# Sliding-window attention with a channel mix on one core: the tail loads of batch 0 moved ahead of the second run loads, and a new order of all engines

## The chip, the cores and the metric

The kernel runs on one core of a Trainium2 chip. A core has five engines that each take their own instructions strictly in the order in which the program hands them over: TensorE (PE in the profile; its weight loads are PEld), VectorE (DVE), ScalarE (ACT), GpSimd (POOL) and SyncE (SP). They wait for each other only by semaphores. SP, ACT and POOL also issue DMA transfers, which 16 DMA engines carry out. The metric is the device time of one execution in microseconds (us), lower is better.

## What is computed

Eight batches of 576 tokens go through causal attention of eight heads of 64 with a window of 128 tokens and a linear (ALiBi) bias, and then through a channel mix as in RWKV. Inputs and output are float32; the kernel works in bfloat16 with float32 sums.

```python
scores = scale * np.matmul(q, k.transpose(0, 1, 3, 2))
mask = (rel >= 0) & (rel < window)          # rel = query position - key position
scores = np.where(mask, scores + bias[None], -1000000000.0)
...
x = attention output, heads side by side     # (8, 576, 512)
x_prev = x moved on by one token
xk = mu_k * x + (1.0 - mu_k) * x_prev
xr = mu_r * x + (1.0 - mu_r) * x_prev
k = np.maximum(xk @ w_k, 0.0)                # 512 -> 1024
v = k * k @ w_v                              # 1024 -> 512
r = 1.0 / (1.0 + np.exp(-(xr @ w_r)))        # 512 -> 512
return (r * v).astype(np.float32)
```

## The kernel before

**The work of one batch.** Heads are handled in four pairs (g = 0 to 3), two pairs at a time (c = 0 and 1) from batch 1 on. For batches 1 to 7 q and k come into `raw` (line 568, four loads each batch), VectorE transposes them into `qt` (line 1157), TensorE makes the scores in two halves per c (line 1190) into the two double banks `duo`, ScalarE takes the exponential (line 1211), VectorE multiplies by a mask that holds the bias and the window (line 1224). The product with V, with a column of ones for the sum, is line 803; reciprocal and division are lines 809 and 814. For batches 1 to 3 the result goes back through TensorE (line 841) and a copy (line 717) into `xt`, with channels on the partitions; from batch 4 on a DMA of SyncE transposes it (line 889). VectorE then forms the difference to the token before (`dl`, line 867) and from it `xk` and `xr` (line 874), four channel groups each.

The channel mix is cut into row pieces: batch 0 in tokens 0 to 255 and 256 to 511, then for each pair of batches the rest. One piece needs eight blocks of line 956 (xk times w_k, four matmuls each, into one of four single banks `uno`), each followed by a relu on ScalarE (line 963) and a square on ScalarE (line 927) or VectorE (line 929), whichever the planner finds free. Then, for each 128 tokens, a block of line 974 (xr times w_r, four matmuls) with a tanh on ScalarE (line 981), two blocks of line 990 (squares times w_v, four matmuls each), and the product of both on VectorE (line 995), which SyncE sends out (line 1020).

**Batch 0 is special.** To start early, its q and k come in by small loads: tokens 0 to 255 through `qx` on the queues of SP and ACT (line 581); tokens 256 to 511 as "run" loads on GpSimd's queue (line 543), first q and k of heads 0 to 3, then of heads 4 to 7; and the last 64 tokens of all heads as two "tail" loads into `ts` (line 561). The runs are transposed on TensorE by line 1051 pair by pair, the tails by line 904 for all pairs together, after which VectorE copies them into `tt`. The second of the two score pieces of each pair in this part reads `tt` (line 747). The bias of batch 0 is added on TensorE by a product with `sid` and `dist` (line 734).

**What sets the order.** Every step is a node of a planner (class `Plan`) with engines that may run it, a cost, dependencies, buffers that it takes and gives back, and a priority. `plan.run` goes through a modelled time and starts on each engine the ready node of best priority; the nodes are then emitted in the order of their starts, and this fixes the order of the instructions on every engine, since the program is built without another scheduler. The priority of a node is its place in the pipeline plus a number from the table `NUDGE`, looked up by the node's number (`rank`, lines 432 to 444). The loads on GpSimd's queue are chained in the order of the string `LOADS` (line 220), one letter for each step of `load_step` (lines 624 to 651): `v` and `V` are halves of V of batch 0, `K` and `k` halves of w_k, `2` and `3` the runs of heads 0 to 3 and 4 to 7, `t` the tails, `a`, `b`, `c` batch 1, `R`, `W`, `w` the other weights. TensorE also gets 90 products of a zero tile (line 708), of lowest priority, wherever the planner has nothing else for it at the start.

Each load on GpSimd's queue signals one of eight semaphores in turn and, from the ninth on, waits until the load that used the same semaphore before has landed.

Of the kernel before, what the change touches and what calls it, by code (L numbers as in the profile page):

```python
# [182 lines left out]
def kernel(  # L183
# [36 lines left out]
    LOADS = 'vK23tVkabRcWw'  # L220
# [106 lines left out]
    def dve_t(n, fast=1):  # L327
# [347 lines left out]

    for what in LOADS:
        load_step(what)
# [618 lines left out]
```

## Time and profile before

| | us |
|---|---|
| median of three runs | 227.17 |
| lowest and highest | 226.61 and 227.76 |
| the profiled execution | 226.8 |
| its span in the trace | 225.0 |
| TensorE busy in it | 215.5 |

The span runs from the first to the last instruction of the trace; the execution's own time is 1.8 us longer. In the lines of the profile a group such as `L956 PE MATMUL uno<-xk,wk_sb` names the line of the kernel, the engine, what is written and what is read; in the timeline the first two numbers are start and duration in us, and the bracket says how long the engine stood idle just before and what ended that.

### The profile page before, as it was taken

To read this page: it belongs to the slowest core of one execution; us is meant where nothing else is said; L and a number is where in the kernel's file an instruction comes from. 1 tells how busy PE (TensorE), PEld (TensorE's weight loads), DVE (VectorE), ACT (ScalarE), POOL (GpSimd) and SP (SyncE) were. 2 spreads that over 40 slices of the span, in tenths; PEclk is the share of its full clock that TensorE was granted. 3 is DMA by queue.
4 is the path that set the end of the run, shared out by engine and by line. 5 is a ranking of instruction groups with operands and counts; after the bars stand their busy time and mean duration, and the time that the engine had idled before them with its cause. 6 is when DMAs were issued, how large, how long until landed. Compare 5 with 4: busy or idle time off the path is not lost.

```text
span 225.0 us, 5805 instructions
## 1 busy us (share of the span) xinstructions
PE 215.5 (96%) x2309; PEld 128.5 (57%) x2339; DVE 195.3 (87%) x378; ACT 167.9 (75%) x319; POOL 58.5 (26%) x88
## 2 busy tenths in 40 slices
PE   8999978999999999999999999999999999999994
PEld 8575736656755555464774545445674455456642
DVE  7387999999999999999998999999999966993432
ACT  3669999498998689967996997676996884527511
POOL 8758535456101900070005600190000000000000
PEclk9999999999999999999999999999999999999999
DMA  6999999999981996189354993599871315141023
GB/s 162 187 166 200 195 155 207 191 189 188 232 166 50 97 209 154 50 56 145 115 69 45 249 188 84 134 153 186 151 108 29 144 47 117 33 144 62 0 93 140
DMA packets 66298, 29.74 MB, mean 132 GB/s; under 512 B 53976, under 2 KB 58336, under 8 KB 66272
## 3 DMA queue, kind: packets, MB, share of 16 engines
q0 software_dynamic: 46832, 16.26, 66.6%
q1 hardware_dynamic: 17696, 12.53, 19.9%
q10 hardware_dynamic: 1744, 0.59, 1.1%
q8 instruction: 18, 0.29, 0.5%
q14 instruction: 8, 0.07, 0.1%
HBM read 33.56 MB, written 9.44 MB: 191 GB/s over the span
## 4 chain that ended last, share of the span: by engine, by line
PE 88%; DVE 3%; ACT 3%; DMA 3%; issue 1%; SPq 1%; DVEq 0%; ACTq 0%
PE uno L990 27%; PE uno L956 27%; PE uno L974 13%; PE duo L803 7%; PE duo L1190 6%; DMA qx<-in_q_dram 3%; PE uno L841 2%; PE uno L708 1%; PE duo L734 1%; PE uno L803 1%; DVE qt L1157 1%; PE duo L747 1%; SPq L581 1%; ACT rl L963 1%; DVE xk L874 1%
## 5 line engine op out<-in xcount | busy, mean ns | idle before, releaser
L956 PE MATMUL uno<-xk,wk_sb 128*128 128x256 bf16 (+2 forms) x410 | 70.4, 313 | 1.2 <-ACT rs L981 0.3
L990 PE MATMUL uno<-wv_sb,kk 128*128 128x512 bf16 (+2 forms) x281 | 67.1, 373 | 1.2 <-issue 0.6
L1211 ACT ACTIVATE at<-duo 128x1024 bf16<-128x1024 f32 x56 | 55.2, 1040 | 13.6 <-PE duo L1190 13.5
L963 ACT ACTIVATE rl<-uno 128x256 bf16<-128x256 f32 (+2 forms) x104 | 47.0, 478 | 12.2 <-PE uno L956 10.9
L956 PEld LDWEIGHTS <-wk_sb 128*128 128x128 bf16 x416 | 38.8, 98 | 22.8 <-issue 1.8
L990 PEld LDWEIGHTS <-kk 128*128 128x128 bf16 x296 | 27.0, 98 | 29.9 <-issue 2.3
L1224 DVE TENSOR_TENSOR at<-at,mask 128x1024 bf16<-128x1024 bf16 x56 | 37.1, 685 | 1.4 <-ACT at L1211 1.2
L547 POOL DMA_DIRECT2D vs<-in_v_dram x32 | 28.5, 905 | 36.4 <-PE duo L803 29.0
L974 PE MATMUL uno<-wr_sb,xr 128*128 128x512 bf16 x135 | 35.1, 379 | 0.5
L927 ACT ACTIVATE kk<-rl 128x256 bf16<-128x256 bf16 (+2 forms) x74 | 35.1, 517 | 0.5
L1157 DVE STREAM_TRANSPOSE qt<-raw 128x576 f32<-128x576 f32 x28 | 33.4, 1236 | 0.0
L981 ACT ACTIVATE rs<-uno 128x512 bf16<-128x512 f32 x36 | 21.6, 616 | 14.0 <-PE uno L974 13.9
L995 DVE SCALAR_TENSOR_TENSOR ot<-rs,uno 128x512 f32<-128x512 bf16 (+2 forms) x37 | 24.2, 664 | 7.6 <-ACT rs L981 4.6
L874 DVE SCALAR_TENSOR_TENSOR xr<-dl,mu_sb,xt 128x576 bf16<-128x576 bf16 (+1 forms) x32 | 24.6, 771 | 0.1
L874 DVE SCALAR_TENSOR_TENSOR xk<-dl,mu_sb,xt 128x576 bf16<-128x576 bf16 (+1 forms) x32 | 24.5, 776 | 0.1
L803 PEld LDWEIGHTS <-at 128*128 128x128 bf16 x576 | 21.4, 98 | 4.9 <-issue 0.8
L814 DVE TENSOR_TENSOR xu<-duo,rc 128x640 bf16<-128x640 f32 x28 | 22.7, 817 | 0.5 <-PE uno L841 0.3
L974 PEld LDWEIGHTS <-xr 128*128 128x128 bf16 x144 | 13.5, 98 | 14.5 <-issue 0.4
L1190 PE MATMUL duo<-qt 32*128 32x256 bf16 (+2 forms) x560 | 18.1, 250 | 1.1 <-ACT at L1211 0.9
L803 PE MATMUL duo<-vs,at 128*128 128x65 bf16 x448 | 18.8, 194 | 0.3 <-ACT at L1211 0.3
L1190 PEld LDWEIGHTS <-qt 32*128 32x128 bf16 x560 | 11.7, 92 | 11.7 <-issue 9.4
L929 DVE TENSOR_TENSOR kk<-rl 128x256 bf16<-128x256 bf16 (+2 forms) x30 | 10.0, 337 | 8.5 <-ACT rl L963 8.0
(73 smaller groups left out, 159.6 us busy)
## 6 DMA issues: line engine op xcount, KB each, us to landing
out_dram<-ot SPq DMA_DIRECT2D x34, 256.0 KB, 2.5
vs<-in_v_dram POOLq DMA_DIRECT2D x32, 128.0 KB, 9.5
raw<-in_q_dram POOLq DMA_DIRECT2D x14, 288.0 KB, 8.8
raw<-in_k_dram POOLq DMA_DIRECT2D x14, 288.0 KB, 9.3
wk_sb<-in_moe_w_k_dram POOLq DMA_DIRECT2D x2, 512.0 KB, 7.8
wv_sb<-in_moe_w_v_dram POOLq DMA_DIRECT2D x2, 512.0 KB, 11.5
qx<-in_k_dram ACTq DMA_DIRECT2D x4, 128.0 KB, 5.1
qx<-in_q_dram SPq DMA_DIRECT2D x4, 128.0 KB, 4.8
```

What stands on the lines that cost most here:

```text
L547: return dma(POOL, 256, issue_t(1024), lambda e: nc.gpsimd.dma_start(out=vs_buf[h.idx][:, j, :, 0:D], in_=v[b, :, 128 * j:128 * j + 128].r ...
L803: nc.tensor.matmul(a[:, hl, t - t0], lhsT=at[:, lo:lo + 128], rhs=vs[:, u, 2 * g + hl, :] if u < NF else tvb[:, 2 * g + hl], start=(u == u ...
L874: lambda e: nc.vector.scalar_tensor_tensor(out=buf[hk.idx][:, g, e0 + c0:e0 + c1], in0=dls(), scalar=mu[:, g:g + 1], in1=xc(1), op0=ALU.mu ...
L927: nc.scalar.activation(out=out, in_=in_, func=AF.Square)
L956: nc.tensor.matmul(one(hp)[:, 0:n], lhsT=wk_sb[:, po, 128 * fo:128 * fo + 128], rhs=xk_buf[hx.idx][:, po, c0:c1], start=(po == 0), stop=(p ...
L963: a = op(ACT, act_t(n), [s], pr, lambda e, hp=hp, hr=hr: nc.scalar.activation(out=rl_buf[hr.idx][:, 0:n], in_=one(hp)[:, 0:n], func=AF.Rel ...
L974: nc.tensor.matmul(one(hp), lhsT=xr_buf[hx.idx][:, po, 128 * c:128 * c + 128], rhs=wr_sb[:, po], start=(po == 0), stop=(po == NPO - 1))
L990: nc.tensor.matmul(one(hv)[:, a:b], lhsT=kk_buf[hk.idx][:, fo, o:o + 128], rhs=wv_sb[:, fo, a:b], start=(fo == 0), stop=(fo == NFO - 1))
L1157: nc.vector.transpose(out=qt_buf[hq.idx][:, S * i:S * i + S].rearrange("p s t -> p (s t)").bitcast(FP32) .rearrange("p (q t) -> p t q", t=TB),
L1190: nc.tensor.matmul(two(hps[j // 2])[:, j % 2, c0:c0 + n], lhsT=qt[r:r + 32, S + 128 * u:S + 128 * u + 128, t], rhs=qt[r:r + 32, q0:q0 + n, t],
L1211: lambda e, ah=ah, j=j: nc.scalar.activation(out=ah(), in_=two(hps[j]), func=AF.Exp, scale=float(scale)), (), [hps[j]])
L1224: nc.vector.tensor_tensor(out=a, in0=a, in1=m, op=ALU.mult)
```

## The change

Two things are changed and nothing else. In `LOADS` the letter `t` moves ahead of `3`: the tail loads of batch 0 are issued between the two pairs of its run loads. And the table `NUDGE` is replaced by another (931 entries before, 865 after, 4 of them equal). The nodes, their costs and their dependencies stay, but for the chain of the four loads that change places.

```diff
-    LOADS = 'vK23tVkabRcWw'
+    LOADS = 'vK2t3VkabRcWw'
...
     NUDGE = {
-        647: 9.44, 648: 14.18, 650: 28.28, 651: -0.02, 652: 28.26, 654: 14.18, 655: 14.18, 656: -0.02, 657: 4.7, 658: 23.5, 659: 14.12, 660: 9.48,
-        661: 4.72, 662: -4.8, 663: 4.72, 664: -4.82, 665: 14.14, 666: -4.82, 667: 9.46, 668: 9.42, 669: 9.38, 670: 28.24, 671: 9.42, 672: 18.76,
...
+        649: 9.36, 650: 4.76, 651: 9.36, 652: -0.02, 653: 0.02, 654: 4.72, 655: -0.04, 656: 9.3, 657: 18.78, 659: 28.22, 660: -4.72, 661: -4.72,
+        662: 4.64, 663: 0.04, 665: 0.02, 666: 4.58, 667: -4.74, 668: -4.76, 669: 4.64, 671: 14.14, 672: -4.76, 673: -0.04, 674: 14.14, 675: -0.1,
...
     }
```

With this the order of instructions is another on TensorE, VectorE, ScalarE and SyncE from the fifth microsecond on; on GpSimd only the four loads change places. TensorE keeps the same number of each kind of instruction. VectorE has 384 steps of the planner instead of 378 and ScalarE 317 instead of 323, since squares and copies may go to either. Line numbers of the new program are five lower behind the table; in this text all lines are those of the kernel before.

147 rows, old and new, of the table NUDGE are left out of this document.

## The prediction

> **What bounds the kernel now.** First the page: busy shares, the 40 slices and the chain that ended last.
>
> ```profile
> span 225.0 us, 5805 instructions
> PE 215.5 (96%) x2309; PEld 128.5 (57%) x2339; DVE 195.3 (87%) x378; ACT 167.9 (75%) x319; POOL 58.5 (26%) x88
> ...
> PE   8999978999999999999999999999999999999994
> ...
> DVE  7387999999999999999998999999999966993432
> ACT  3669999498998689967996997676996884527511
> ...
> PE 88%; DVE 3%; ACT 3%; DMA 3%; issue 1%; SPq 1%; DVEq 0%; ACTq 0%
> ```
>
> TensorE carries 88% of the chain, and only its first slices are not full. To see where it is not, the view by stretches (columns: PE, PEld, DVE, ACT, POOL busy, clock, DMA):
>
> ```profile
> 15.00:26.00 11.00, 10.29 (x187) 6.43 (x186) 9.66 (x27) 10.56 (x29) 6.68 (x10) 1.00 1.39 192
> 26.00:33.20 7.20, 5.89 (x94) 3.83 (x89) 7.12 (x14) 7.13 (x15) 2.73 (x5) 1.00 2.08 161
> 33.20:43.00 9.80, 8.87 (x138) 6.46 (x140) 9.45 (x21) 7.97 (x17) 5.13 (x7) 1.00 1.24 205
> 43.00:51.20 8.20, 8.09 (x85) 4.69 (x88) 8.18 (x15) 6.05 (x11) 4.29 (x7) 1.00 1.90 184
> 51.20:221.80 170.60, 168.80 (x1659) 96.02 (x1684) 151.10 (x254) 128.80 (x237) 27.92 (x41) 1.00 0.70 117
> ```
>
> Three regimes. From 26 to 33.2 us VectorE (7.12 of 7.20) and ScalarE (7.13) are both full and TensorE is idle for 1.31 us: these two are the bound there. From 33.2 to 43 TensorE still loses 0.93. From 51.2 on it loses 1.80 in 170.6 us, about 1%. All matmuls are the same before and after, so a new order can win only idle: 0.71 + 1.31 + 0.93 + 0.11 to 51.2 us, 1.80 later, 4.9 us in all; and a delay up to 43 us reaches the end undiminished, since TensorE then has no slack to take it up. [...]
>
> **The change, part by part.** *The loads.* On GpSimd's queue the two tail loads (ts) go ahead of the second pair of run loads (raw) of batch 0. Nothing is added: the same four issues, in another order.
>
> ```profile
> 6.44 0.77 POOL L543 DMA_DIRECT2D raw<-in_q_dram  x1
> 7.17 0.78 POOL L543 DMA_DIRECT2D raw<-in_k_dram  x1
> 7.90 0.67 POOL L561 DMA_DIRECT2D ts<-in_q_dram  x1
> 9.08 0.61 POOL L561 DMA_DIRECT2D ts<-in_k_dram  x1 [0.51 <-DMA vs<-in_v_dram]
> ...
> 17.07 0.53 POOL L568 DMA_DIRECT2D raw<-in_k_dram  x1 [1.94 <-DMA raw<-in_k_dram]
> 17.33 0.32 PE L1051 MATMUL uno<-ident,raw 64*64 64x64 bf16 x16
> ...
> 17.57 0.59 PE L904 MATMUL uno<-ident,ts 128*64 128x64 bf16 x16
> ```
>
> The ninth load on GpSimd's queue waits for the landing of the first (the 0.51 us). In the new order that wait falls on the last run load: it issues at 9.08 instead of 7.17, 1.9 us later, and the tails 1.4 to 1.9 earlier. Landing is another matter: the run load landed at 17.0 (the wait of 1.94 ends with it), both tails were there at 17.57, behind it. If landing follows the order on the queue, the four swap places inside 17.6, and pairs 2 and 3 are transposed at about 17.6 instead of 17.33. Bounds: 0, and +1.9 if landing moves as far as the issue. I take 0, for the rows put all four landings within a few tenths before 17.6. What is queued behind on GpSimd are the loads of batch 1, whose first wait (1.94 us) then names a tail instead of a run; weights and V follow in the old order, so nothing later moves by this. Below zero: the tails come early, but their copies stood ready in time before, and ScalarE and VectorE, full, set the pace.
>
> *The order up to the scores of batch 1's second half.* I compared the instruction orders of both programs engine by engine. Ahead of the first L1190 of heads 4 to 7, TensorE executes the same set in both. On ScalarE the sets ahead of its exponentials differ by three small copies and squares that trade places with VectorE, about 0.05 us. As ScalarE is full there, this point stays where it is:
>
> ```profile
> 25.41 2.33 DVE L1157 STREAM_TRANSPOSE qt<-raw 128x576 f32<-128x576 f32 x2
> ...
> 29.16 1.25 DVE L1157 STREAM_TRANSPOSE qt<-raw 128x576 f32<-128x576 f32 x1
> ...
> 31.25 1.94 ACT L1211 ACTIVATE at<-duo 128x1024 bf16<-128x1024 f32 x2
> ...
> 33.25 0.64 PE L1190 MATMUL duo<-qt 32*128 32x256 bf16 x16 [0.19 <-DVE qt L1157]
> ```
>
> The new VectorE order runs the second pair of transposes back to back, which ends it at 29.16 + 2 x 1.17 = 31.5 instead of 33.2. It gains nothing: the scores also wait for both banks of the duo tiles, free when the exponentials end at 33.19.
>
> *The order from 33.9 to 43.* Here lies the difference that I can price. Before, TensorE goes on with three L956 blocks. After, it has an L974 first, which reads xr of all four pairs, and VectorE reaches the last of these after two dl, two masks, three xr and two xk.
>
> ```profile
> 33.71 1.00 DVE L874 SCALAR_TENSOR_TENSOR xk<-dl,mu_sb,xt 128x320 bf16<-128x320 bf16 x2
> 34.03 1.98 ACT L1211 ACTIVATE at<-duo 128x1024 bf16<-128x1024 f32 x2
> 34.63 3.10 DVE L1224 TENSOR_TENSOR at<-at,mask 128x1024 bf16<-128x1024 bf16 x5
> ...
> 36.06 0.64 PE L1190 MATMUL duo<-qt 32*128 32x256 bf16 x24
> ...
> 37.24 2.02 ACT L1211 ACTIVATE at<-duo 128x1024 bf16<-128x1024 f32 x2
> ```
>
> From 31.5: 2 x 0.62 for the masks, 5 x 0.50 for xr and xk, 2 x 0.30 for dl (an estimate from the 0.50 of the wider operation) make 4.3, so 35.8. TensorE, free at 33.9, waits 1.9 us, against 0.93 of idle in that stretch before: +1.0. Against it: before, ScalarE squeezes five pieces of L963 and L927 between the exponentials that end at 36.0 and those that start at 37.24; after, two. That takes back about half of 1.24, say 0.5. The blocks that TensorE does until the first transpose L841 of batch 1 are others, but worth the same:
>
> ```profile
> 41.38 0.55 PE duo L803 x18
> 41.92 0.86 PE uno L990 x4
> ...
> 45.92 0.87 PE uno L956 x8
> 46.80 0.88 PE uno L974 x4
> ```
>
> Before: six L956 at 0.44, one L974, three L803, two L990: 2.64 + 0.88 + 1.65 + 1.72 = 6.89. After: three, two, four and two: 1.32 + 1.76 + 2.20 + 1.72 = 7.00. Step: +1.0 - 0.5 = **+0.5 us**; bounds -0.9 (all idle of this stretch gone) and +1.9.
>
> *After 51 us.* Ahead of the first scores of batch 4 both orders have the same number of TensorE blocks, two exchanged. Five squares and one copy's choice of engine move to other places (L927 runs 69 times, L929 35), hidden behind TensorE. I take the 1.80 us of idle as unchanged; bounds 0 and twice that. The last five blocks of TensorE are the same, so what lies behind the last matmul stays.
>
> Sum: 226.8 for the profiled execution (span 225.0 and 1.8 around it) + 0.5 = 227.3. The median of the three runs, 227.17, is 0.37 above the profiled one, so 227.3 + 0.37 = **227.7 us**.
>
> **The rivals.** *ScalarE becomes the bound at 43 to 48 us (slower).* The new order pushes five L956 blocks between the four L841 of batch 1, ahead of the scores of batch 2; before, only two stood there.
>
> ```profile
> 39.05 1.04 ACT L963 ACTIVATE rl<-uno 128x256 bf16<-128x256 f32 x3
> 39.84 0.83 ACT L927 ACTIVATE kk<-rl 128x256 bf16<-128x256 bf16 x2
> 45.96 0.64 ACT L717 COPY xt<-uno 128x576 bf16<-128x576 bf16 x1 [0.53 <-PE uno L841]
> 51.15 0.64 PE L1190 MATMUL duo<-qt 32*128 32x256 bf16 x24
> ```
>
> TensorE needs 5 x 0.44 + 4 x 0.29 = 3.4 for them, ScalarE 4 x 0.64 + 5 x 0.35 + 5 x 0.41 = 6.4, and with four uno banks TensorE can't run far ahead. The L990 and the scores behind (0.86 and 0.6) cover 1.5 of the 3.0; the rest, 1.5, is lost: 229.2. For it: ScalarE was idle 2.15 us from 43.0 to 51.2 because its work had been done earlier, and now is not. Against: overlap of its instructions makes the true cost less (three L963 start within 0.79 us). It decides once ScalarE enters this stretch later than TensorE, that is when the wait at 33.9 exceeds my 1.9.
>
> *The new order fills the holes (faster).* L974 and L990 cost ScalarE less per microsecond of TensorE than L956, and the new order has more of them at 34 to 41. If the wait of 1.9 is no wait (xr early), 0.9 goes there and half of the 1.31 before: 227.17 - 0.9 - 0.65 = 225.6.
>
> *The later order is worse (slower).* The idle after 51.2 doubles: 227.17 + 1.8 = 229.0. For it: everything is permuted; against: the handovers keep their distances. Behind the last attention block of the last batch stand 10 blocks of TensorE instead of 12 until its first L956, but VectorE takes that block's normalisation at once instead of after several others.
>
> *The swap does harm (slower).* The run load lands 1.9 later, and ScalarE, full from 15 us, hands all of it on: 229.1. That is also how the change could fail to do what it says: the tails early, but nothing waiting for them.
>
> *The clock.* It was 1.00 in every stretch above, with 1.31 us idle in 7.2. [...]
>
> **How the numbers follow.** Forecast 0.44, ScalarE's knot 0.22, later order worse 0.10, late run load 0.06 (slower 0.38 together), holes filled 0.18. 0.5% of 227.17 is 1.1 us, about what a measurement of this kernel can tell from no change: faster is below 226.0, slower above 228.3. The forecast's own range is 226.1 to 228.3. The one for 8 in 10 takes in the rivals on both sides: 225.6 to 229.3.
>
> **What would show it.** Right: L904 ahead of the L1051 of pairs 2 and 3, those at about 17.6; the first L1190 of heads 4 to 7 at 33 to 33.6; a wait of TensorE on an xr of VectorE after it; the L1190 of batch 2 that stood at 51.15 at about 51.6, one L990 owing or not; idle after it near 1.8. Wrong: a wait for raw beyond 18.5; waits on ScalarE (rl, kk, xt) at 43 to 48; no wait at 34; over 3 us of idle after 51.

## The result, and the profile after

The changed kernel takes 229.91 us (median of 4 executions, 228.18 to 230.46); the kernel before took 227.12 beside it (226.61 to 227.76). The ratio is 1.011, 95% interval 1.0073 to 1.0147: slower, where 227.7 with a range of 225.6 to 229.3 had been forecast. The profiled execution took 229.43, its span 227.5. From here on line numbers are those of the kernel that is spoken of: in the changed one and in all that are built on it they are five lower than before (L1185 is the scores line L1190, L1206 the exponential L1211, L969 is L974, L951 is L956, L985 is L990).

The page of the changed kernel, shares and slices as before:

```profile
span 227.5 us, 5822 instructions
PE 215.9 (95%) x2309; PEld 127.8 (56%) x2339; DVE 197.1 (87%) x384; ACT 166.4 (73%) x313; POOL 59.1 (26%) x88
...
PE   7899958999999999999999999899999999999994
...
PEclk9999988999999999999999999999999999999999
...
PE 85%; ACT 5%; DMA 5%; DVE 2%; issue 1%; ACTq 1%; DVEq 0%
```

TensorE is busy for as long as before (215.9 against 215.5) in a span 2.5 us longer. New are two 8 in the row of the granted clock, in the sixth and seventh slice, and ScalarE with 5% of the chain. The same five stretches as before, the last one now up to 224 us, in the view by stretches (PE, PEld, DVE, ACT, POOL busy, clock, DMA share, GB/s):

```profile
15.00:26.00 11.00, 10.42 (x203) 7.04 (x202) 9.62 (x28) 10.56 (x29) 7.07 (x10) 1.00 1.38 193
26.00:33.20 7.20, 4.41 (x72) 2.98 (x72) 6.92 (x12) 6.43 (x15) 2.94 (x5) 0.92 2.04 159
33.20:43.00 9.80, 9.11 (x108) 5.16 (x108) 8.28 (x18) 8.05 (x13) 4.94 (x7) 0.88 1.25 205
43.00:51.20 8.20, 8.01 (x105) 5.71 (x106) 7.95 (x14) 6.82 (x18) 4.85 (x8) 1.00 1.88 193
51.20:224.00 172.80, 170.49 (x1666) 96.63 (x1691) 153.93 (x264) 127.22 (x231) 27.82 (x40) 1.00 0.71 116
```

From 26 to 33.2 us TensorE now idles for 2.79 us instead of 1.31, and ScalarE, which was full there (7.13), has 0.77 us free. From 33.2 to 43 TensorE looks busier than before (9.11 against 8.87) with fewer matmuls (108 against 138): the clock was 0.88, so each took longer. What happened is seen in the timelines (start, duration, group; the bracket is the idle time ahead and what ended it). ScalarE before:

```profile
28.55 1.99 ACT L1211 ACTIVATE at<-duo 128x1024 bf16<-128x1024 f32 x2
30.38 0.81 ACT L717 COPY xt<-uno 128x320 bf16<-128x320 bf16 x2
```

ScalarE after:

```profile
29.09 1.03 ACT L1206 ACTIVATE at<-duo 128x1024 bf16<-128x1024 f32 x1
29.99 0.44 ACT L712 COPY xt<-uno 128x320 bf16<-128x320 bf16 x1
30.30 1.06 ACT L1206 ACTIVATE at<-duo 128x1024 bf16<-128x1024 f32 x1
32.09 1.94 ACT L1206 ACTIVATE at<-duo 128x1024 bf16<-128x1024 f32 x2 [0.73 <-PE duo L1185]
```

and TensorE after:

```profile
28.13 0.64 PE L1185 MATMUL duo<-qt 32*128 32x256 bf16 x16 [0.17 <-DVE rc L804]
28.78 0.34 PE L836 MATMUL uno<-ident,xu 128*128 128x128 bf16 x3
31.41 0.64 PE L1185 MATMUL duo<-qt 32*128 32x256 bf16 x24 [2.30 <-ACT at L1206]
...
32.74 2.77 PE L969 MATMUL uno<-wr_sb,xr 128*128 128x512 bf16 x6 [0.22 <-issue]
35.44 0.65 PE L1185 MATMUL duo<-qt 32*128 32x256 bf16 x16
```

TensorE before, at the same block:

```profile
29.68 0.29 PE L1190 MATMUL duo<-qt 32*128 32x256 bf16 x2 [0.27 <-ACT at L1211]
30.59 0.64 PE L1190 MATMUL duo<-qt 32*128 32x256 bf16 x22 [0.62 <-ACT at L1211]
```

The scores of batch 1 go into two double banks, and the second scores block writes bank 0 first. Before, ScalarE emptied bank 0 and then bank 1, back to back. In the new order it empties bank 1, then makes a copy of `xt`, and then empties bank 0: the waiting block of TensorE can't start until the last of the three is done, and TensorE stands for 2.30 us, after three small matmuls, where before it waited 0.27 and 0.62. ScalarE in turn waits 0.73 us for those scores. Behind them six L969 take 2.77 us, where seven take 1.90 at full clock (e14, below). The granted clock microsecond by microsecond (PE busy, clock, DMA share, GB/s):

```profile
32.00:33.00 1.00, 0.78 (x9) 0.55 2.62 135
33.00:34.00 1.00, 1.00 (x3) 0.50 1.81 184
34.00:35.00 1.00, 1.00 (x4) 0.50 1.30 194
35.00:36.00 1.00, 1.00 (x18) 0.74 1.25 208
```

The clock is halved for 0.90 + 1 + 1 + 0.52 = 3.42 us. With that the first scores of heads 4 to 7 are at 35.44 instead of 33.25. The loads did what the forecast said; GpSimd's queue and TensorE's products with the loaded tiles:

```profile
6.35 0.67 POOL L556 DMA_DIRECT2D ts<-in_q_dram  x1
6.98 0.65 POOL L556 DMA_DIRECT2D ts<-in_k_dram  x1
...
9.32 0.77 POOL L538 DMA_DIRECT2D raw<-in_k_dram  x1 [0.91 <-DMA vs<-in_v_dram]
...
16.03 0.44 PE L899 MATMUL uno<-ident,ts 128*64 128x64 bf16 x16 [0.37 <-ACT qk L712]
17.81 0.49 PE L1046 MATMUL uno<-ident,raw 64*64 64x64 bf16 x32
```

Much later there is one more wait that was not there before: VectorE can't write an `xu` buffer of batch 5, since the DMA that transposes its last content hasn't ended, and the scores behind wait 0.74 us for it:

```profile
144.29 0.82 DVE L809 TENSOR_TENSOR xu<-duo,rc 128x640 bf16<-128x640 f32 x1 [1.33 <-DMA xt<-xu]
...
145.17 0.64 PE L1185 MATMUL duo<-qt 32*128 32x256 bf16 x16 [0.74 <-DVE xu L809]
```

### The profile page after: what moved, and what is told of

Its sections match the earlier page's. It is cut to its first block, busy times and chain, and to the rows that moved or that the text cites. A ratio compares the mean times of both kernels' runs of the same rounds, so it can differ in the third digit from the quotient of the medians.

```text
span 227.5 us, 5822 instructions
## 1 busy us (share of the span) xinstructions
PE 215.9 (95%) x2309; PEld 127.8 (56%) x2339; DVE 197.1 (87%) x384; ACT 166.4 (73%) x313; POOL 59.1 (26%) x88
## 4 chain that ended last, share of the span: by engine, by line
PE 85%; ACT 5%; DMA 5%; DVE 2%; issue 1%; ACTq 1%; DVEq 0%
PE uno L985 26%; PE uno L951 26%; PE uno L969 13%; PE duo L1185 7%; PE duo L798 6%; DMA qx<-in_k_dram 3%; DMA xt<-xu 2%; PE uno L836 2%; ACT at L1206 2%; PE uno L703 1%; PE duo L729 1%; DVE xu L809 1%; ACT xt L712 1%; PE uno L798 1%; PE duo L742 1%
## 5 line engine op out<-in xcount | busy, mean ns | idle before, releaser
L951 PE MATMUL uno<-xk,wk_sb 128*128 128x256 bf16 (+2 forms) x412 | 71.3, 313 | 0.3
L985 PE MATMUL uno<-wv_sb,kk 128*128 128x512 bf16 (+2 forms) x280 | 67.2, 373 | 0.8 <-issue 0.2
L1206 ACT ACTIVATE at<-duo 128x1024 bf16<-128x1024 f32 x56 | 55.9, 1044 | 10.2 <-PE duo L1185 10.1
L951 PEld LDWEIGHTS <-wk_sb 128*128 128x128 bf16 x416 | 38.4, 98 | 22.0 <-issue 1.2
L985 PEld LDWEIGHTS <-kk 128*128 128x128 bf16 x296 | 27.4, 98 | 30.3 <-issue 1.3
L969 PE MATMUL uno<-wr_sb,xr 128*128 128x512 bf16 x134 | 36.8, 392 | 0.8 <-issue 0.2
L976 ACT ACTIVATE rs<-uno 128x512 bf16<-128x512 f32 x36 | 22.1, 617 | 19.3 <-PE uno L969 16.2
L922 ACT ACTIVATE kk<-rl 128x256 bf16<-128x256 bf16 (+2 forms) x69 | 34.1, 528 | 0.7
L990 DVE SCALAR_TENSOR_TENSOR ot<-rs,uno 128x512 f32<-128x512 bf16 (+2 forms) x37 | 24.4, 666 | 6.1 <-PE uno L985 5.7
L969 PEld LDWEIGHTS <-xr 128*128 128x128 bf16 x144 | 13.5, 100 | 14.6 <-issue 1.8
L1185 PE MATMUL duo<-qt 32*128 32x256 bf16 (+2 forms) x560 | 17.8, 250 | 4.0 <-ACT at L1206 2.9
L1185 PEld LDWEIGHTS <-qt 32*128 32x128 bf16 x560 | 11.9, 92 | 14.7 <-issue 12.2
L924 DVE TENSOR_TENSOR kk<-rl 128x256 bf16<-128x256 bf16 (+2 forms) x35 | 11.7, 335 | 9.3 <-ACT rl L958 8.5
```

Source lines behind the costliest of these rows:

```text
L922: nc.scalar.activation(out=out, in_=in_, func=AF.Square)
L951: nc.tensor.matmul(one(hp)[:, 0:n], lhsT=wk_sb[:, po, 128 * fo:128 * fo + 128], rhs=xk_buf[hx.idx][:, po, c0:c1], start=(po == 0), stop=(p ...
L969: nc.tensor.matmul(one(hp), lhsT=xr_buf[hx.idx][:, po, 128 * c:128 * c + 128], rhs=wr_sb[:, po], start=(po == 0), stop=(po == NPO - 1))
L985: nc.tensor.matmul(one(hv)[:, a:b], lhsT=kk_buf[hk.idx][:, fo, o:o + 128], rhs=wv_sb[:, fo, a:b], start=(fo == 0), stop=(fo == NFO - 1))
L1185: nc.tensor.matmul(two(hps[j // 2])[:, j % 2, c0:c0 + n], lhsT=qt[r:r + 32, S + 128 * u:S + 128 * u + 128, t], rhs=qt[r:r + 32, q0:q0 + n, t],
L1206: lambda e, ah=ah, j=j: nc.scalar.activation(out=ah(), in_=two(hps[j]), func=AF.Exp, scale=float(scale)), (), [hps[j]])
```

## The experiments

Theory A: TensorE idles behind ScalarE's order at 29 us, the clock is halved behind that idle time, and the rest follows from being late. B: the new order's waits cost their own time, wherever they stand, and the clock is a by-product. C: the four loads. The kernels change the list of nodes between planner and emission: `order` is what `plan.run` returned, `at[n]` the node of number n, and `put(a, b)` moves node a right behind node b (`put(a, b, 0)`: right ahead of it). Node 867 is the exp of bank 0, 869 that of bank 1, 744 the copy of `xt`, 871 TensorE's second scores block of batch 1. Single executions at full clock and with a halved stretch are told apart by the mean granted clock of the whole execution: 3.42 us at half clock in 227 make 0.992. "Fallen" means a mean under 0.995. The mean doesn't tell where the clock fell. That is seen only in the five profiled executions that fell (the change, e6, e8, e9, e13), and there it was between 30.3 and 32.1 us each time; for all others the place is an inference. The kernel before is fallen in 8 of 99 executions beside these runs.

### One cause at a time

**e1: the old loads in the new order.**

```diff
+        put(85, 93)
+        put(87, 85)
```

> The changed kernel with its four loads back in the old order on GpSimd's queue, every other engine's order unchanged. Theory A (TensorE stands idle from 28.9 to 31.4 us behind ScalarE and its clock is then halved for 3.4 us): the loads play no part, 229 to 230.5, same wait of about 2.3 us at the second L1185 block. Theory C (the loads: the last run load now lands later and ScalarE, full from 15 us, hands the delay on): 228 or less, and the wait shrinks.

Measured: 229.56 with all six executions, 229.34 without the longest (232.32), which the ratio leaves out: 1.0129 [1.0092, 1.0167]. The loss stays, so C falls as its cause. Fallen in 3 of 6. The profiled execution (229.34) was at full clock, and is late all the same: TensorE waits the 2.30 us, 0.9 us for the tail loads and 0.6 for an xr, and there are two stalls on `xu`, TensorE's only idle times of note after 130 us:

```profile
144.05 0.64 PE L1185 MATMUL duo<-qt 32*128 32x256 bf16 x16 [0.42 <-DVE xu L809]
172.08 0.63 PE L1185 MATMUL duo<-qt 32*128 32x256 bf16 x16 [0.98 <-DVE xu L809]
```

**e2: the idle time filled.** 36 products of the zero tile `warm` into a single bank that is free, ahead of the waiting block. ScalarE's order stays.

```diff
+            if n.seq == 871:
+                for _ in range(36):
+                    nc.tensor.matmul(uno[1][:, 0:128], lhsT=warm, rhs=warm, start=True, stop=True)
```

> The changed kernel with 36 products of the zero tile (0.056 us each, 2.0 us) put on TensorE into the idle stretch before the second L1185 block. Nothing that it waits for comes earlier. Theory A: the granted clock stays 1.00, and the time falls by 1.5 to 2.2 us to about 228. Theory B (the order alone costs the time by its waits, the clock is a by-product that falls into a stretch where TensorE waits anyway): 229 to 230.5 as the changed kernel, clock 1.00 or not.

Measured: 227.14, ratio 1.0027 [1.0011, 1.0044], 0 of 12 fallen. The waiting block starts at 30.97, 2.65 us behind the start of the three L836 (28.32); in the change it is 2.63. The wait has not been shortened; only the idle time is filled:

```profile
28.50 2.17 PE L1268 MATMUL uno<-warm 128*128 128x128 bf16 x36
30.97 0.64 PE L1185 MATMUL duo<-qt 32*128 32x256 bf16 x24 [0.30 <-ACT at L1206]
...
34.86 1.04 PE L969 MATMUL uno<-wr_sb,xr 128*128 128x512 bf16 x4 [0.59 <-DVE xr L869]
```

Useless work on TensorE takes most of the loss away: the ratio falls by 0.0083 against the change's and 0.0068 against e13's, some 1.9 and 1.5 us, the 1.5 to 2.2 that A gave. B, by which only the block's start counts, can't explain this. It is not all the clock, however, since executions of the change at full clock lose time as well (see "The rest of the loss").

**e3: the exp of bank 0 first, the copy last.**

```diff
+        put(867, 869, 0)
```

> The changed kernel with only ScalarE's order altered in one place: the two exponentials of batch 1's first scores run bank 0 first and back to back, the copy into xt behind them instead of between. Theory A: TensorE's wait falls from 2.3 to about 1.2 us (bank 0 is free 1.2 us earlier, the block starts on it), the clock stays at 1.00, time about 227.5 (1.7 for the clock, 0.7 for the wait). Theory B: only the wait counts, 0.3 to 0.7 us less than the changed kernel, 229.2 or more.

Measured: 227.82, ratio 1.0066 [1.0045, 1.0087], 1 of 6 fallen: near A's 227.5, though A had the clock at full speed throughout, and far from B's 229.2. The 2.30 us wait is split into 0.82 and 0.62 us. Now the wait on xr is seen that the forecast had priced:

```profile
35.19 1.04 PE L969 MATMUL uno<-wr_sb,xr 128*128 128x512 bf16 x4 [1.16 <-DVE xr L869]
```

**e4: the wait put into the kernel before.** Its exp of bank 0 goes behind the copy.

```diff
+        put(867, 744)
```

> The kernel before with the suspected cause put in: the exponential that frees bank 0 runs last, behind the other one and one copy, all else as before. Theory A: a TensorE wait of about 2 us arises at the second L1190 block, the clock drops to 0.5 for 3.4 us in most executions, time 229 or more (1.0 for the wait, 1.7 for the clock). Theory B: +0.3 to +1.0, at most 228.2.

Measured: 227.23, ratio 1.0046 [1.0022, 1.0071]. TensorE waits 1.52 us there instead of 0.27 and 0.62. 5 of 12 are fallen, with a median of 228.52; the other 7 have 226.87. By the median this is B's number (at most 228.2) and not A's 229: the loss that A expected for most executions came in fewer than half of them. Fallen executions are 1.65 us longer than the others. The profiled one did not fall, so that the clock falls behind this wait is not seen, only likely.

### How much idle time, how often

**e8: a longer wait.** The exp of bank 1 is computed twice.

```diff
+            if n.seq == 867:
+                at[869].emit(n.eng)
```

> The changed kernel with the exp of bank 1 computed twice, so that the exp of bank 0 comes 1.07 us later and TensorE is idle for some 3.4 us instead of 2.3. Theory A (how long TensorE is idle sets how often the clock falls: 2 of 23 executions with .6 us, 5 of 12 with 1.5, 6 of 10 with 2.3): the clock falls in nearly every execution, and none is at 1.000; median 231.0 to 231.8, ratio 1.020 to 1.025. Rival B (the fall is by chance and doesn't follow the gap): as often as now, about 6 of 10, median some 1.1 over the 229.6 of e1 and 229.9 of the change, and single executions at 1.000 near 229.3.

Measured: 230.6, ratio 1.0171 [1.0149, 1.0193], 4 of 4 fallen: more often, as A said, at a time 0.4 us under its range. The profiled execution lost two stretches in a row (PE busy, clock):

```profile
30.00:31.00 1.00, 0.00 (x0) 0.66 2.27 163
...
37.00:38.00 1.00, 1.00 (x14) 0.92 1.18 213
```

From 30.32 to 37.16 are 6.84 us, twice 3.42.

**e9: the long wait in the kernel before.** The edits of e4 and e8 together, in the old order and with the old loads.

> The kernel before, its own order and loads, with the exp of bank 0 behind the copy of xt (e4) and the exp of bank 1 computed twice ahead of it, so that TensorE waits some 2.6 us at the second scores block of batch 1 where e4 had 1.5. Theory A (the wait itself, in whichever order, lowers the clock): the clock falls in 5 to 8 of 10 executions, 228.9 to 229.8 in these and near 227.9 in the others, median 228.5 to 229.6, ratio 1.008 to 1.014, so that the old order loses what the change lost. Rival B (the new order loses it, whatever the wait): 227.2 to 227.9, ratio up to 1.006, and the clock falls in 5 of 12 at most.

Measured: 228.86, ratio 1.0079 [1.0054, 1.0103], 3 of 6 fallen (median 229.32; the others 228.14), at the lower edge of what A gave. The wait is 2.42 us, with the halved clock behind it:

```profile
31.18 1.04 PE L1190 MATMUL duo<-qt 32*128 32x256 bf16 x24 [2.42 <-ACT at L1211]
32.16 3.07 PE L974 MATMUL uno<-wr_sb,xr 128*128 128x512 bf16 x8
```

So the old order with such a wait loses most of what the new one loses. Not all of the 0.8% is the clock's: the executions at full clock are 1.3 us above the median beside them (226.82), since here the block comes late and ScalarE has a microsecond more work; the fallen ones have 1.2 us more.

**e14 and e11: half the filling.** 18 zero products instead of 36, which leave 1.05 and 1.31 us of wait. e14 has the change's own `xu` buffers; e11 takes two others for batch 5:

```diff
+        at[1490].need[0].idx, at[1454].need[0].idx = 2, 3
```

> The changed kernel with 18 zero matmuls in the gap and its own xu buffers. Theory A (separate terms): the xu stall of .4 to .7 us stays, 227.5 to 228.0, ratio 1.003 to 1.006, clock 1.000. Rival B (the stall comes only when TensorE was late before it, as e2 without a stall had it): 226.9 to 227.2, ratio 1.000 to 1.002, no wait on xu.

> e10 with 18 of the 36 zero matmuls in the gap: some 1.1 us of it filled and 1.2 us idle behind it. Theory A (how long TensorE stands idle sets how often the clock falls): 2 to 4 of 12, median 227.2 to 227.7, ratio 1.003 to 1.005. Rival B (any matmul in the gap holds the clock): 0 of 12, 227.1 as e7. Rival C (the gap has to be full): 6 of 10 as in e10, median as e10.

Measured: e14 226.90, ratio 1.0009 [0.9991, 1.0027]; e11 227.05, 1.0005 [0.9990, 1.0021]; 0 of 24 fallen. With 18 useless matmuls the change can't be told from the kernel before. Of e14's theories it is the second that holds: one stall on `xu` is left, of 0.17 us. In e11 and e14 no execution fell. For e11 A gave 2 to 4 of 12, and its rival B (any matmul in the gap holds the clock) gave what came: none, and 227.1. In e15 below, with the same filling, 3 of 12 did fall, which speaks against B if they fell at this place. The timeline of e14 stands beside the change's above line by line:

```profile
29.19 1.17 PE L1268 MATMUL uno<-warm 128*128 128x128 bf16 x18
31.41 0.64 PE L1185 MATMUL duo<-qt 32*128 32x256 bf16 x24 [1.05 <-ACT at L1206]
31.99 1.90 PE L969 MATMUL uno<-wr_sb,xr 128*128 128x512 bf16 x7
33.82 0.88 PE L1185 MATMUL duo<-qt 32*128 32x256 bf16 x16
35.30 1.04 PE L969 MATMUL uno<-wr_sb,xr 128*128 128x512 bf16 x4 [0.59 <-DVE xr L869]
```

The waiting block starts at 31.41 in both. At the scores of heads 4 to 7 the change is 1.62 us behind, and there is nothing between but the clock.

**e12: filling in the kernel before** (36 zero products, as e2).

> The kernel before with the 36 zero matmuls at the same place, ahead of its second scores block of batch 1, where it waits .27 + .62 us for the two exps. Theory A (its few executions with a fallen clock, 4 of 48, come from this place): no execution under 0.997; but 36 matmuls take 1.9 us, 1.0 more than the waits there, and TensorE has .18 and .34 us of waits soon behind to make up for it: 226.6 to 227.4 median, ratio 1.001 to 1.004. Rival B (what TensorE loses there is ScalarE's and VectorE's anyway): 226.3 to 226.6, ratio 0.999 to 1.000, and the best of all kernels by its mean.

Measured: 228.97, ratio 1.0099 [1.0069, 1.0129], 1 of 6 fallen; a miss of its own making. In the old order the bank that the zero products write is the one that the copy of `xt` reads; so they came late and then held up the scores:

```profile
30.82 2.17 PE L1273 MATMUL uno<-warm 128*128 128x128 bf16 x36 [1.50 <-ACT xt L717]
32.92 0.63 PE L1190 MATMUL duo<-qt 32*128 32x256 bf16 x24
```

It says nothing of the rare fallen executions of the kernel before. It does show that this block some 2 us late, at full clock, costs about as much (2.15 over the median beside it).

### The rest of the loss

**e10 and e13: the `xu` buffers alone, and the change again,** the latter on the chip of e14.

> The changed kernel with nothing mended but the two xu buffers of batch 5. Theory A (the stall at 139 to 152 us costs what it shows, and the clock falls at 30 us as before): the clock falls in about 6 of 10, 228.6 to 229.2 in these and 227.2 to 227.8 in the others, median 228.3 to 229.0, .7 to 1.3 less than e1 and the change. Rival B (VectorE or the DMA has the time anyway, the stall comes back at another place): 229.4 to 229.9, no difference from the change.

> The changed kernel itself, unmended, on the chip of the next three. Theory A (gap with clock and xu stall are separate, and each costs what it shows): 229.0 to 230.0, ratio 1.010 to 1.014, the clock fallen in about 6 of 10 executions. Rival B (most of it is the gap with its clock, the stall costs .5 us at most): 228.2 to 228.8, as e10's 1.0062.

Measured: e10 228.10, ratio 1.0062 [1.0042, 1.0083], 8 of 11 fallen, a little under A's time; e13 229.18, ratio 1.0095 [1.0069, 1.0122], 4 of 6 fallen, A's time. So the buffers are worth some 0.3 to 0.5% while the idle time is there, and with the idle time half filled nothing (e14 against e11). In e10 the fallen executions (median 228.17) are only 0.3 us above the others (227.88); in e13 it is 0.8. e13 is 2.28 us over e14. In the two profiles the scores of batch 2 start at 48.75 and 47.63, which is 1.12 us; the last scores at 184.87 and 182.87; of the 0.88 between, 0.83 are e13's stalls on `xu` less e14's:

```profile
144.72 0.64 PE L1185 MATMUL duo<-qt 32*128 32x256 bf16 x16 [0.42 <-DVE xu L809]
172.35 0.64 PE L1185 MATMUL duo<-qt 32*128 32x256 bf16 x16 [0.58 <-DVE xu L809]
```

Lateness alone does not set the stall. In e1, at full clock, the scores of batch 2 start at 48.08, earlier than in e13, and its stalls are the longest, 1.40 us; in e3 they start at 47.33, earlier than in e14, and it stalls for 0.43 us. Last scores are 1.73 us later in e1 than in e14 (184.60 and 182.87): 0.45 of it is there at the scores of batch 2, and 1.23 is the difference of the stalls. So an execution at full clock can lose more than a microsecond at `xu`. What makes the transposing DMA late for VectorE is open.

**e5 and e15: the loads, in either order.** e5 is the kernel before with the new loads, e15 is e11 with the old ones.

```diff
+        put(84, 95)
+        put(88, 84)
```

> The kernel before with nothing changed but the four loads on GpSimd's queue: the tail tokens of batch 0 come between the two pairs of the second-half runs, as in the change, and every engine keeps the order of before. Theory A (the change lost its time at the exp of bank 0 and through the clock, not at the loads): the wait on ts at the V blocks, .7 us between 15 and 20 us, gets shorter; L1051 on the second pair of runs starts near 17.8 instead of some .9 earlier, and VectorE has other work there; 226.2 to 226.8, ratio 0.999 to 1.002, clock 1.000 in nearly every execution. Rival C (the later run load costs by itself): qt of batch 1 comes later and heads 0 to 3 start later; 227 to 228, ratio 1.003 to 1.007.

> e11 (18 zero matmuls, new xu buffers) with the four loads on GpSimd's queue in the old order. Theory A (the new loads gain a little in this order, since VectorE's and TensorE's order is made for them): .2 to .5 us over e11's, 227.2 to 227.5, ratio 1.002 to 1.004, with a wait on ts at the V blocks. Rival B (the loads don't matter): as e11, 1.0005.

Measured: e5 226.80, ratio 1.0011 [0.9996, 1.0026], no difference; e15 227.74, ratio 1.0064 [1.0036, 1.0092], 3 of 12 fallen, 227.61 without these; more than either theory gave. The old order can't use the early tails. The new one needs them: with the old loads, pairs 2 and 3 are transposed at 18.59, behind tails that come in two pieces, against 17.61 in e11, and 0.6 us of that arrives at the end.

```profile
16.94 0.32 PE L899 MATMUL uno<-ident,ts 128*64 128x64 bf16 x8 [0.25 <-DMA ts<-in_k_dram]
18.59 0.45 PE L1046 MATMUL uno<-ident,raw 64*64 64x64 bf16 x32
```

**e6, e7, e16: can the new order be made better than before?** e6: exp of bank 0 first, other `xu` buffers, and on VectorE 715, 717 and 716 right behind 761. e7: the last two with the 36 zero products. e16: exp of bank 0 first, 12 zero products, other `xu` buffers.

> The changed kernel with three places mended: the exp of bank 0 ahead of that of bank 1 with the copy of xt behind both; on VectorE the delta and the two xr of heads 4 to 7's projection (L862, L869 x2) ahead of a mask product and one xk, so that the 1.2 us wait of TensorE at L969 near 34 us goes; and two xu buffers of batch 5 that are not in use any more (2 and 3 instead of 0 and 1), so that the stall of .4 to 1.3 us at 139 to 152 us goes. Theory A (what is left of e3's 1.0066 are these two waits): 1.2 + .4 less than the 227.6 of e3, 226.0 to 226.4, ratio 0.998 to 1.001, clock 1.000. Rival B (the work that is pulled ahead pushes the mask products behind it, and the second scores or values of heads 0 to 3 wait instead): 227.0 to 227.6, ratio 1.003 to 1.006.

> The changed kernel with the 36 zero matmuls in the 2.3 us gap (e2) and the last two mends of e6 (xr earlier on VectorE, other xu buffers), but the exp of bank 0 still last. It has the whole wait on the exp, and none of the clock's loss. Theory A: e2's 227.14 less its .6 us wait on xr, 226.4 to 226.7, ratio 1.000 to 1.002, clock 1.000 in all executions. Rival B (the wait at the exp itself costs its 2.3 us less what ScalarE makes up): not under 227.0, ratio over 1.003.

> The changed kernel with the exp of bank 0 first (e3), 12 zero matmuls (.7 us) into the wait of .8 to 1.0 us that is left there, and the new xu buffers. Theory A (gap, clock and stall were all that the change lost, and the order is otherwise as good as before): clock 1.000 in all executions, heads 4 to 7's first scores near 33.2, 226.3 to 226.7, ratio 0.998 to 1.001. Rival B (the 1.2 us wait on xr at 34 that e3 showed is a loss of the new order by itself): 227.0 to 227.6, ratio 1.002 to 1.005.

Measured: e6 228.0, ratio 1.0058 [1.0030, 1.0087], 4 of 8 fallen; e7 227.15, 1.0021 [1.0009, 1.0033], 0 of 11; e16 227.09, 1.0008 [0.9991, 1.0025], 0 of 12. None beats the kernel before. e6 lies above both of its theories, and its fallen and other executions have the same median (228.0); e7 lies between its two. The move on VectorE missed its aim: one of the three nodes makes an xk, the last xr still stands behind a mask product, and the wait on xr in e7 is 0.77 us. e16 has it in full, with its scores of heads 4 to 7 earlier (33.08) than in the kernel before (33.25), and ends where that ends:

```profile
33.08 0.88 PE L1185 MATMUL duo<-qt 32*128 32x256 bf16 x16
35.12 1.04 PE L969 MATMUL uno<-wr_sb,xr 128*128 128x512 bf16 x4 [1.16 <-DVE xr L869]
```

That wait is thus mostly made up later. Its time is Rival B's and its ratio Theory A's, so e16 does not decide between them.

## Why the prediction was wrong, point by point

- **The loads, 0.** Right: tails ahead of the runs (16.03), pairs 2 and 3 at 17.81, forecast 17.6, and no difference by themselves (e5). That the new order depends on them (e15) was not said.
- **"As ScalarE is full there, this point stays where it is"** (the first scores of heads 4 to 7, at 33.25). This is the step that failed. The sets of work ahead of that point were compared, and they are the same; the order within the sets was not. Which of two banks is emptied first decides when TensorE may go on, and ScalarE, full before, itself came to wait 0.73 us for scores. With the clock held the point is at 33.82 (e14), which is 0.57 late and too little to show in the median. With the halved clock it is at 35.44, 2.19 late.
- **The clock.** It was a paragraph without a chance. The longest wait forecast was 1.9 us, and that the clock holds through one of that length was not shown: in the kernel before TensorE's longest wait at these scores was 0.62 us. The wait that came was 2.30 us, at a place where none was forecast, and 3 of 4 executions have a fallen clock (7 of 10 with e13). Two things were missing: the wait, and that the clock can fall with one of this length. It was halved in the profiles of e9 (2.42 us), the change (2.30), e13 (2.29) and e6 (0.99 and 0.62), and stayed at 1.00 in those of e1 (2.30) and e10 (2.05).
- **The wait on xr, 1.9 us.** It is there, with 0.59 us (e2, e14) or 1.16 (e3, e16), and in the change itself hidden by the slow matmuls ahead. The step's +0.5 us stands close to what the filled kernels e2 and e14 lose in all (1.0027 and 1.0009, which is 0.6 and 0.2 us). At the mark that the forecast set, the second scores of batch 2 (51.15 before), these are at 50.90 in e14 and 52.13 in the change, with one L985 block of 0.86 us still owing in both (24 weight loads from `kk` ahead of it instead of 28): 0.6 us late with the clock held, 1.8 with it halved.
- **After 51 us, unchanged.** Not quite: 2.31 us idle in 172.8 instead of 1.80, the 0.74 on `xu` among it. The forecast's bound of twice 1.80 held it. That the stall comes and goes between kernels whose order behind 51 us is the same (none in e2, 1.00 us in e13) was not foreseen.
- **The rivals.** ScalarE's knot at 43 to 48 is not there: TensorE idles 0.19 us from 43 to 51.2 instead of 0.11. The holes were not filled, and the late run load didn't come. The range's slower end was built from mechanisms that did not happen, and the time passed it by another. By how much was in part chance: the one of four executions at full clock, 228.18, lies inside the range.

How the loss divides is shown in part. In their profiles e13 and e14, which differ by 18 zero products, are 1.12 us apart at the scores of batch 2, behind the halved clock, and the stalls on `xu` add 0.83. Among the executions of the change itself (with e13), the 7 fallen ones have a median of 229.58 and the 3 at full clock (228.18, 228.51, 228.89) one of 228.51, so the clock is worth some 1.1 us there. Those three are still 1.6 us above e14's median of 226.90, and none of them was profiled. e1's profile, at full clock, has 1.4 us of stalls on `xu`; whether the same holds for these, and why the filling takes that part away too, stays open.

## What to carry to other kernels

Where two orders have the same work ahead of a point, follow the buffers as well: a consumer that empties a pair of banks in the wrong order, with one more piece in between, holds the producer for the whole (here 2.30 us instead of 0.27 and 0.62). Price a TensorE wait by the work around it, not only by its length: in a thin stretch of small matmuls, waits of 1.5 to 2.4 us went with executions that were 0.8 to 2.2 us longer at a fallen clock (e10: 0.3), and that in some executions only, so a median of few executions can miss it. Eighteen zero products in such a wait are a cheap way to see whether the idle time costs more than the wait itself; compare executions at one clock as well, for the filling took away more than the clock's part here.

## What the runs showed of the hardware

The halved stretch, worked out from the view by microseconds, was 3.42 us long in the change and in e6, e9 and e13, and 6.84 in e8. It didn't start at a fixed distance from the idle time: TensorE's wait began at 29.11 us in the change and 29.02 in e13, and the clock fell at 32.10 and 31.46; in e6 it fell at 30.70, while the wait was on. In the stretch of about the same length (3.41 us) just ahead of each fall TensorE was not idle all the time: it was busy for 1.10 us in the change and e13, 1.99 in e6, 1.58 in e8 and 0.79 in e9. How often the clock fell goes with the least busy time of TensorE in any stretch of 3.4 us, again about as long as the halved one (steps of 0.2 us from 27.6 to 32, in the profile of each kernel; the change, e6, e9 and e13 are left out, since slowed matmuls count as busy for longer (2.77 us for six L969, where seven take 1.90); e8's profile fell too, but TensorE did next to nothing in its stretch):

| least busy time in 3.4 us | kernels | fallen |
|---|---|---|
| 3.0 | e2, e7 | 0 of 23 |
| 2.2 to 2.3 | before, e5, e16 | 9 of 123 |
| 2.0 | e11, e14, e15 | 3 of 36, all in e15 |
| 1.5 to 1.7 | e3, e4, e12 | 7 of 24 |
| 1.0 | e1, e10 | 11 of 17 |
| 0.2 | e8 | 4 of 4 |

The four kernels left out have 14 fallen of 24. The longest single wait orders the rows nearly as well (0.30 us in e2 and e7, 0.6 in the kernel before, e5 and e16, 1.05 to 1.31 in e11, e14 and e15, 0.82 to 1.52 in e3, e4 and e12, 2.05 and 2.30 in e10 and e1, 3.22 in e8). Whether the busy share decides or the wait is therefore not shown; no run varied one with the other held.
